# A fused attention and mixture-of-experts kernel: the identity in a tile of its own, other constants loaded later, and the first routing phase's PSUM and id tiles rearranged

## The chip, the core and the metric

One NeuronCore of a Trainium2 chip runs the program; the metric is the device time of one execution in microseconds (us). The engines are TensorE (PE in the profile, with its weight loads as PEld), VectorE (DVE), ScalarE (ACT), GpSimd (POOL) and SyncE (SP, which here issues most of the transfers).

## The reference

Three stages, in fp32:

```python
# 1. attention over a window of 64, B=4, H=8, S=576, D=64; x is (2304, 512)
scores = where(0 <= i - j < 64, q @ k.T / 8, -1e9)
x = softmax(scores) @ v
# 2. eight experts, each takes at most 288 tokens; all 2304*8 logits are
#    visited in falling order, a token goes to the first expert with room
logits = x @ w_gate
order = argsort(-logits.flatten())
out[mask_e] = relu(x[mask_e] @ w1[e]) @ w2[e]
# 3. a dense block with a leaky ReLU
h = out @ w_in
return maximum(0.01 * h, h) @ w_out
```

## The kernel before, in words

**Attention** (`attention`, lines 63 to 268) goes through 18 chunks of 128 tokens. One turn `i` of its main loop issues: `scores(i)` (mask products at line 121, then q times k at line 130, into the PSUM tile `as`), the row maxima on DVE (lines 137, 138), the gate products `stage_g` in every third turn (line 93, from the load `avt`), the exponentials on ACT (line 145), `values(i-2)` (line 165, into the PSUM tile `ao`; for the last two chunks into a tile of the tag `as`), `stage_gt` (transposes of the gate products against the identity, line 107; DVE copies them into the value tile `avo`, line 108, and POOL copies that into `ave`, lines 110 and 112), `sums(i-2)` (lines 170 to 176, then `done(c)`, then the normalisation at line 181), and `trans(i-1)` (transposes of the exponentials against the identity, line 150, copied out at line 152). For the last three chunks the normalisation runs on ACT, eight instructions for each chunk at line 185, as the last work of the stage.

The loads go out on SP in one written order. `early()` runs after the first two loads and `late()` after six. `early()` also starts the load of `cft`, all fp32 constants with the identity among them, on ACT's queue. `late()` issues two more constant loads (`cit`, and `cbt` beyond its first 128 columns) on SP, and calls `Router.start` (line 343). That puts seven small instructions into DVE's queue ahead of the first row maximum; three of them read constants: line 347 reads `cft`, line 349 reads `cft`, line 350 reads the late part of `cbt`. Every engine works through its own queue in order.

**Routing** (`Router`). The eight experts are filled in eight phases. Phase 0 finds its threshold digit by digit in six rounds. A round counts on PE how many logits lie above each candidate (19 small matmuls into a PSUM tile `rq`: one for what is left of the experts' room, 18 for the chunks, which multiply the comparison grid `r_G` by the one-hot choice `r_oh`), DVE clips the count (`r_sat`, a scan), PE sums it up (`rp`), and DVE builds the next comparisons (three instructions on `r_G`, then `r_E`). The first round's grid and one-hot are made ahead, chunk group by chunk group, in `ahead` (line 361; groups of 6, 6, 3 and 3 chunks), and so are the integer keys (`keys`, line 388; results `r_k`, `r_M`, `r_E`). `ahead` and `keys` are generators: two steps are taken per turn of the attention, the rest in one go at the end. After the six rounds phase 0 places the chosen tokens and turns slot numbers into row ids: two DVE products into `r_OB` (nine chunks each), after each of them nine matmuls into one PSUM tile, then `r_ip`, one matmul, and `r_ids`. Each matmul reads 128 columns of `r_OB` from its chunk's start on, that is beyond its own 18 columns.

The attention's PSUM pool has all eight banks: the tag `as` four, `apt` two and `ao` two. After it, `m_pa` (tag `acc`, four banks), `rps` (tag `rp`, one), `pm` (tag `xt`, one) and `m_ph` (two) take the banks over. Phase 0's counts are tiles of the tag `acc`.

**Experts and the dense block** (`Moe`). After phase 0's ids, three gathers fetch expert 0's rows (`xg`), PE runs warm-up products meanwhile (`warm`, `WARM`), transposes the rows (`xtp`) and starts expert 0. The later phases are interleaved with the matmuls by a planner in the program (`Clocks`, `RouteDriver`): it adds up modelled times for each engine, starting after the attention, and issues a routing or weight-conversion piece when the model says that its inputs are there. Whether expert 1's gather has been issued by step 6 (`self.soon`) decides if its rows are transposed beside expert 0's matmuls or only after a forced `R.finish(1)`.

Of the kernel before, what the change touches and what calls it, by code (L numbers as in the profile page):

```python
# [6 lines left out]
F32 = mybir.dt.float32  # L7
# [10 lines left out]
NT = 18  # L18
# [260 lines left out]
def consts_np():  # L279

    f, i, b = {}, {}, {}
    p = np.arange(128, dtype=np.float32)[:, None]
# [9 lines left out]
    f['tid'] = 128 * np.arange(18, dtype=np.float32) + p - IDC  # L292
    f['ident'] = np.eye(128, dtype=np.float32)
    j = np.arange(128)[:, None] % 18
# [18 lines left out]
class Router:  # L313
# [3 lines left out]
    def __init__(self, nc, pool, pp, L, cf, ci, cb, ones_b, pow2):  # L317
# [19 lines left out]
        self.G = [pool.tile([128, n * NT], BF, name=f"r_G{k}") for k, n in enumerate((128, 38))]  # L337
        self.OB = pool.tile([128, 18 * 17 + 128], F16, name="r_OB")
        for x in self.G + [self.OB]:
            nc.gpsimd.memset(x, 0.0)  # L340
        self.ip = pool.tile([128, 128], F16, name="r_ip")
    def start(self):
        v, cf = self.nc.vector, self.cf
        v.memset(self.base, 0.0)
        v.memset(self.sat, 0.0)
        v.memset(self.ip, 0.0)
        v.tensor_copy(self.uw, cf['ew'])
        v.memset(self.slotg, 0.0)
        v.tensor_scalar(out=self.nrem, in0=self.base[:, 0], scalar1=cf['na'], scalar2=cf['nb'], op0=ALU.mult, op1=ALU.add)
        v.tensor_copy(self.comb, self.combb)  # L350
    def ps(self, p, n, apart=False):

        self.nps += 1
        if apart:
            return self.p0.tile([128, 512], F32, tag="acc", name=f"rq{self.nps}", bufs=4)[:p, :n]
        return self.pp.tile([128, 128], F32, tag="rp", name=f"rp{self.nps}")[:p, :n]
# [3 lines left out]
    def ahead(self, a, b):  # L360

        v = self.nc.vector
        if a == 0:
            self.first = [self.t([128, NT], F32, "m", 0), self.t([128, NT, 8], BF, "oh", 0), self.t([128, NT], F32, "mxw", 0)]
            self.ge0, self.win0 = self.grid(0, 128)
            self.e0 = self.t([128, NT], F32, "E", 0)
            self.eqw0 = self.G[1].bitcast(F32)[:, :8 * NT].rearrange("p (c e) -> p c e", e=8)
        m, OH, mxw, eqw = self.first[0][:, a:b], self.first[1][:, a:b], self.first[2][:, a:b], self.eqw0[:, a:b]
        def b3(ap, last):
            return ap.unsqueeze(2).to_broadcast([128, b - a, last])  # L370
        def bm(ap, last):
            return ap.unsqueeze(1).to_broadcast([128, b - a, last])
        ks = self.keys(m, self.e0, a, b, True)
        v.tensor_reduce(out=m, in_=self.Lm[:, a:b], axis=AX.X, op=ALU.max)
        yield True
        v.tensor_tensor(out=eqw, in0=self.Lm[:, a:b], in1=b3(m, 8), op=ALU.is_equal)
        next(ks)
        yield True
        v.tensor_tensor(out=self.ge0[:, a:b, :127], in0=b3(m, 127), in1=bm(self.ci['t1'].bitcast(F32), 127), op=ALU.is_ge)
        next(ks)  # L380
        v.tensor_tensor(out=eqw, in0=eqw, in1=bm(self.cf['ew'], 8), op=ALU.mult)
        next(ks)
        yield True
        v.tensor_reduce(out=mxw, in_=eqw, axis=AX.X, op=ALU.max)
        next(ks)
        yield True
        v.tensor_tensor(out=OH, in0=eqw, in1=b3(mxw, 8), op=ALU.is_equal)
        next(ks)
    def keys(self, m, E, a, b, first):

# [14 lines left out]
        yield  # L405
        v.scalar_tensor_tensor(out=E[:, a:b], in0=M[:, 0], scalar=float(1 << 31), in1=M[:, 1], op0=ALU.add, op1=ALU.add)
        yield
    def grid(self, k, w):
# [3 lines left out]
    def phase(self, ph, out):  # L412
# [26 lines left out]
        if ph < 7:  # L439
            for r in range(6):  # L440
# [6 lines left out]
                for lo, hi in zip(cuts, cuts[1:]):  # L447
# [9 lines left out]
                    if hi == NT:  # L457
# [7 lines left out]
                        elif ph:  # L465
                            E = t([128, NT], F32, "E", f"{ph}_0")
                            for _ in self.keys(m, E, 0, NT, False):
                                pass
                        else:
                            E = self.e0  # L470
# [7 lines left out]
                yield 'v', 1  # L478
                v.tensor_tensor_scan(self.sat[rows], pc[rows], self.ones[rows, :8], 0.0, ALU.max, ALU.min)
                yield 'p', 0  # L480
                pa = self.ps(128, 8)
# [73 lines left out]
        yield 'd', 0  # L555
        OB = self.OB[:, :NT * NT].rearrange("p (c a) -> p c a", a=NT)
        HI = self.G[0].bitcast(F16)[:, :NT * NT].rearrange("p (c a) -> p c a", a=NT)
# [5 lines left out]
        pi = None  # L563
        for lo, hi in ((0, 9), (9, 18)) if ph == 0 else ((0, 18),):
            TT(out=OB[:, lo:hi], in0=HI[:, lo:hi], in1=b3(cf['tid'][:, lo:hi], hi - lo, NT), op=ALU.mult)
            yield 'p', 0
            pi = self.ps(128, 16) if pi is None else pi
            for c in range(lo, hi):
                nc.tensor.matmul(pi, self.OB[:, NT * c:NT * c + 128], LO[:, c], start=(c == 0), stop=(c == NT - 1))
        yield 'v', 1  # L570
# [775 lines left out]
def build(nc, tc, qT, kT, v, vT, wg, cfd, cid, cbd, w12, wio, out):  # L1346
    with ExitStack() as ctx:
        ctx.enter_context(tc.manual_schedule())
        c = ctx.enter_context(tc.tile_pool(name="c", bufs=1))
        dr = ctx.enter_context(tc.tile_pool(name="dr", bufs=1, space=bass.MemoryType.DRAM))  # L1350
        cft = c.tile([128, CFN], F32, name="cft")
        cit = c.tile([128, CIN], I32, name="cit")
        cbt = c.tile([128, CBN - MW], BF, name="cbt")
        cf = {k: cft[:, o:o + n] for k, (o, n) in CFO.items()}
        ci = {k: cit[:, o:o + n] for k, (o, n) in CIO.items()}
        cb = {k: cbt[:, o - MW:o - MW + n] for k, (o, n) in CBO.items()}
        ident = cf['ident']
        ones = c.tile([128, 128], BF, name="ones"); nc.vector.memset(ones, 1.0)

        nc.scalar.activation(cft[:, 0:1], ones[:, 0:1], AF.Exp)  # L1360
        L = c.tile([128, 160], F32, name="L")[:, :NT * 8].rearrange("p (c e) -> p c e", e=8)
# [26 lines left out]
        queue = []  # L1388
        def done(c):
            if c in ahead:  # L1390
                queue.append(rt.ahead(*ahead[c]))
            if c == NT - 1:
                drain()
# [3 lines left out]
        with tc.tile_pool(name="mk", bufs=1) as mk:  # L1397
# [4 lines left out]
            def early():  # L1402
                nc.scalar.dma_start(cft, cfd)
                nc.sync.dma_start(wg_sb, wg)
            def late():
                nc.sync.dma_start(cit, cid)
                nc.sync.dma_start(cbt[:, 128:], cbd[:, MW + 128:].bitcast(BF))
                rt.start()
            attention(nc, tc, ident, cb['ident'], qT, kT, v, vT, wg_sb, maskb, xd, L, filler, early, late, done)
        pa = ctx.enter_context(tc.tile_pool(name="m_pa", bufs=4, space=PSUM, reuse_waits="tile"))  # L1410
        rt.p0 = pa
        rt.pp = ctx.enter_context(tc.tile_pool(name="rps", bufs=1, space=PSUM, reuse_waits="tile"))
        pm = ctx.enter_context(tc.tile_pool(name="pm", bufs=1, space=PSUM, reuse_waits="tile"))
        ph = ctx.enter_context(tc.tile_pool(name="m_ph", bufs=2, space=PSUM, reuse_waits="tile"))
        nc = cv.nc = rt.nc = Clocks(nc)
# [33 lines left out]
```

## Time and profile before

| | us |
|---|---|
| runs of the kernel before | 780.02, 781.0, 3415.35 |
| their median | 781.0 |
| the profiled execution | 781.95 |
| its span, first to last instruction | 780.3 |
| outside the span (difference) | 1.65 |
| PE busy in the span | 735.5 (94%) |
| DVE busy | 438.3 (56%) |
| ACT busy | 334.8 (43%) |
| POOL busy | 173.2 (22%) |

In the rows further down the first number of a timeline or chain row is the start in us from the span's beginning, the second the duration in us (of a merged row: of all its instructions). In brackets stands how long the engine was idle before it, and what ended that. A name such as `as<-ak,aq` is output from inputs.

### The profile page before, as it was taken

Reading aid. Unit: us, or ns where it says so; the run is one execution under the profiler, and the core shown is the slowest. Engines: PE = TensorE matmul, PEld = TensorE weight load, DVE = VectorE, ACT = ScalarE, POOL = GpSimd, SP = SyncE. Lnnn points to the kernel's source line nnn. Section 1 sums busy time; section 2 is a strip of 40 time slices with the busy share of each in tenths; the row PEclk is TensorE's granted clock in tenths of the full one; section 3 lists DMA queues with packets and bytes.
Section 4 is the critical chain, followed back from the end, with each engine's and each line's share of the span. In section 5 each row is a group of like instructions: output and inputs, shape, how many; then the busy total and the mean of one; then the engine's idle time right before and its main releaser. Section 6 shows DMA issues by size and latency. Waiting matters only on the chain.

```text
span 780.3 us, 15243 instructions
## 1 busy us (share of the span) xinstructions
PE 735.5 (94%) x5906; PEld 624.5 (80%) x5906; DVE 438.3 (56%) x1113; ACT 334.8 (43%) x736; POOL 173.2 (22%) x262
## 2 busy tenths in 40 slices
PE   3999649999999999999999999999999999999996
PEld 2777526789777779997778899988889998888895
DVE  2689778989789979987752334222233222222332
ACT  2788824657775534432112445322134532222321
POOL 3434112402000004400000388300018850000201
PEclk9999959999999999999999999999999999999999
DMA  9997128643477556433224365623426452214742
GB/s 346 408 380 271 56 76 310 232 161 108 161 239 252 212 194 219 159 122 130 107 84 163 109 220 165 217 80 136 152 91 220 157 199 104 105 64 173 252 172 98
DMA packets 39943, 138.56 MB, mean 178 GB/s; under 512 B 4926, under 2 KB 5822, under 8 KB 39872
## 3 DMA queue, kind: packets, MB, share of 16 engines
q1 hardware_dynamic: 35136, 123.11, 44.1%
q0 software_dynamic: 4304, 14.16, 5.4%
q8 instruction: 46, 0.75, 0.4%
q10 hardware_dynamic: 432, 0.32, 0.1%
q14 instruction: 25, 0.20, 0.1%
HBM read 117.66 MB, written 19.92 MB: 176 GB/s over the span
## 4 chain that ended last, share of the span: by engine, by line
PE 74%; DVE 17%; DMA 4%; ACT 3%; issue 2%; POOLq 0%; SPq 0%; POOL 0%; DVEq 0%; ACTq 0%
PE h L1262 33%; PE oa L1262 21%; PE ya L1262 10%; DVE r_G L1262 3%; PE rp L1262 3%; DVE w L1262 2%; PE ao L165 2%; DMA cv_in<-in_wio_dram 2%; PE apt L150 1%; DVE cv_r L1262 1%; PE as L130 1%; DVE amx L137 1%; PE xtp L1262 1%; DMA cbt<-in_cb_dram 1%; DVE hh L1262 1%
## 5 line engine op out<-in xcount | busy, mean ns | idle before, releaser
L1262 PE MATMUL h<-Y,w 128*128 128x512 f32 (+1 forms) x600 | 135.2, 371 | 0.0
L1262 DVE SCALAR_TENSOR_TENSOR h<-h,tg 128x512 f32<-128x512 f32 (+1 forms) x80 | 51.6, 644 | 146.9 <-ACT tg L1262 146.7
L1262 PE MATMUL oa<-w,hh 128*128 128x512 f32 x540 | 132.9, 392 | 0.0
L1262 ACT COPY tg<-h 128x512 f32<-128x512 f32 (+1 forms) x80 | 43.5, 543 | 185.4 <-PE h L1262 172.9
L1262 PEld LDWEIGHTS h<-Y,w 128*128 128x128 f32 x600 | 104.3, 189 | 18.4
L1262 PEld LDWEIGHTS oa<-w,hh 128*128 128x128 f32 x540 | 99.7, 188 | 19.8 <-issue 0.2
L1262 POOL TENSOR_TENSOR w<-raw,w 128x512 fp32r<-128x512 f32 x53 | 66.7, 1290 | 206.6 <-DVE xT L1262 111.3
L1262 PE MATMUL ya<-hh,w 128*128 128x288 f32 x672 | 99.8, 296 | 0.6 <-DVE hh L1262 0.6
L1262 PE MATMUL h<-xT,w 128*128 128x288 f32 x672 | 100.0, 297 | 0.0
L1262 PEld LDWEIGHTS h<-xT,w 128*128 128x128 f32 x672 | 92.5, 188 | 0.6
L1262 PEld LDWEIGHTS ya<-hh,w 128*128 128x128 f32 x672 | 92.0, 188 | 0.8 <-DVE hh L1262 0.8
L1262 PE MATMUL h<-Y,res 128*128 128x512 f32 (+1 forms) x360 | 81.7, 371 | 0.0
L1262 PE MATMUL oa<-res,hh 128*128 128x512 f32 x324 | 80.6, 393 | 0.0
L1262 DVE TENSOR_TENSOR hh<-h,hh 128x512 fp32r<-128x512 f32 (+1 forms) x80 | 51.0, 637 | 38.5 <-ACT hh L1262 38.3
L1262 POOL DMA_INDIRECT out_dram<-ot,sidx x18 | 19.5, 1081 | 238.0 <-DVE ot L1262 134.9
L1262 PEld LDWEIGHTS h<-Y,res 128*128 128x128 f32 x360 | 62.5, 189 | 11.0
L1262 ACT CAST hh<-h 128x512 fp32r<-128x512 f32 (+1 forms) x80 | 43.5, 544 | 64.1 <-DVE h L1262 64.1
L1262 PEld LDWEIGHTS oa<-res,hh 128*128 128x128 f32 x324 | 59.5, 188 | 11.9 <-ACT hh L1262 0.4
L1262 ACT ACTIVATE hh<-h 128x288 fp32r<-128x288 f32 (+1 forms) x64 | 26.4, 412 | 91.7 <-PE h L1262 89.5
L1262 ACT CAST w<-raw 128x512 fp32r<-128x512 f32 x112 | 64.1, 620 | 0.0
L1262 DVE SCALAR_TENSOR_TENSOR hh<-h,hh 128x288 fp32r<-128x288 f32 x56 | 25.4, 454 | 63.4 <-ACT hh L1262 63.2
L145 ACT ACTIVATE ap<-as,anm 128x128 f32<-128x128 f32 x144 | 41.6, 396 | 24.3 <-DVE anm L138 16.8
(172 smaller groups left out, 941.5 us busy)
## 6 DMA issues: line engine op xcount, KB each, us to landing
w<-wsp SPq DMA_DIRECT2D x80, 512.0 KB, 3.4
raw<-in_w_dram SPq DMA_DIRECT2D x53, 512.0 KB, 3.9
cv_in<-in_wio_dram SPq DMA_DIRECT2D x32, 512.0 KB, 5.2
wsp<-w SPq DMA_DIRECT2D x20, 512.0 KB, 3.4
avo<-in_v_dram SPq DMA_DIRECT2D x6, 876.0 KB, 8.1
aq<-in_q_dram SPq DMA_DIRECT2D x12, 384.0 KB, 7.5
avt<-in_vt_dram SPq DMA_DIRECT2D x6, 768.0 KB, 8.0
xd<-ax SPq DMA_DIRECT2D x18, 256.0 KB, 7.2
```

The source lines that it names most:

```text
L130: nc.tensor.matmul(S[64 * t:64 * t + 64, a, u, :].rearrange("p (b c) -> p b c", b=2), q[h], k[h], start=False, stop=True, skip_group_check ...
L137: nc.vector.tensor_reduce(out=mx, in_=S[:, a:a + n], axis=AX.X, op=ALU.max)
L145: nc.scalar.activation(p[:, u, :], S[:, a, u, :], AF.Exp, bias=nm[a][:, u:u + 1], scale=0.125)
L150: nc.tensor.transpose(pt[:, u, :], p[:, u, :], ident)
L165: nc.tensor.matmul(o[64 * t:64 * t + 64, h // 4, h % 4, :], ptb[:, u, 64 * t:64 * t + 64], (ve, vo)[t][m][:, s, h, :], start=True, stop=Tr ...
L1262: return f(*a, **kw)
```

## The change

The identity becomes the first 128 columns of the fp32 constants and gets a tile `ident`, which `early()` loads; the other 183 columns stay in `cft` and are loaded in `late()` on SP, between `cit` and `cbt`. `start` keeps only memsets; the three instructions that read constants move to `start2`, called in `sums(4)` by `done(4)`, after chunk 4's logits. In `ahead` the steps of `keys` come later (two of them after `r_oh`), and the last one, which made `r_E` by chunk groups, becomes `rest`: one instruction over all 18 chunks, issued in phase 0's first round behind the scan. Phase 0's counts use the tag `xt` of the pool `pm`. `r_OB` becomes two tiles, and phase 0 puts its first nine chunks into the one and the other nine into the other.

```diff
-    f, i, b = {}, {}, {}
+    f, i, b = {'ident': np.eye(128, dtype=np.float32)}, {}, {}
...
-        self.OB = pool.tile([128, 18 * 17 + 128], F16, name="r_OB")
-        for x in self.G + [self.OB]:
+        self.OB = [pool.tile([128, 18 * (n - 1) + 128], F16, name=f"r_OB{n}") for n in (9, 18)]
+        for x in self.G + self.OB:
             nc.gpsimd.memset(x, 0.0)
...
         v.memset(self.ip, 0.0)
+        v.memset(self.slotg, 0.0)
+    def start2(self):
+        v, cf = self.nc.vector, self.cf
         v.tensor_copy(self.uw, cf['ew'])
-        v.memset(self.slotg, 0.0)
         v.tensor_scalar(out=self.nrem, ...
         v.tensor_copy(self.comb, self.combb)
...
-            return self.p0.tile([128, 512], F32, tag="acc", name=f"rq{self.nps}", bufs=4)[:p, :n]
+            return self.p0.tile([128, 4, 96], F32, tag="xt", name=f"rq{self.nps}", bufs=1).rearrange("p a b -> p (a b)")[:p, :n]
...
         v.tensor_tensor(out=eqw, in0=self.Lm[:, a:b], in1=b3(m, 8), op=ALU.is_equal)
-        next(ks)
         yield True
         v.tensor_tensor(out=self.ge0[:, a:b, :127], ...
-        next(ks)
+        yield True
...
         v.tensor_tensor(out=OH, in0=eqw, in1=b3(mxw, 8), op=ALU.is_equal)
+        yield True
         next(ks)
+        next(ks)
...
-        v.scalar_tensor_tensor(out=E[:, a:b], in0=M[:, 0], scalar=float(1 << 31), in1=M[:, 1], op0=ALU.add, op1=ALU.add)
-        yield
+    def rest(self, E):
+        self.nc.vector.scalar_tensor_tensor(out=E, in0=self.M[:, 0], scalar=float(1 << 31), in1=self.M[:, 1], op0=ALU.add, op1=ALU.add)
...
                 v.tensor_tensor_scan(self.sat[rows], ...
+                if ph + r == 0:
+                    self.rest(E)
...
-        for lo, hi in ((0, 9), (9, 18)) if ph == 0 else ((0, 18),):
-            TT(out=OB[:, lo:hi], in0=HI[:, lo:hi], ...
+        for k, (lo, hi) in enumerate(((0, 9), (9, 18)) if ph == 0 else ((0, 18),)):
+            ob = self.OB[(k + (ph > 0)) % 2]
+            TT(out=ob[:, :NT * (hi - lo)].rearrange("p (c a) -> p c a", a=NT), in0=HI[:, lo:hi], ...
...
-                nc.tensor.matmul(pi, self.OB[:, NT * c:NT * c + 128], LO[:, c], ...
+                nc.tensor.matmul(pi, ob[:, NT * (c - lo):NT * (c - lo) + 128], LO[:, c], ...
...
+            if c == 4:
+                rt.start2()
...
-                nc.scalar.dma_start(cft, cfd)
+                nc.scalar.dma_start(ident, cfd[:, :128])
                 nc.sync.dma_start(wg_sb, wg)
             def late():
                 nc.sync.dma_start(cit, cid)
+                nc.sync.dma_start(cft, cfd[:, 128:])
                 nc.sync.dma_start(cbt[:, 128:], cbd[:, MW + 128:].bitcast(BF))
...
-        rt.p0 = pa
...
+        rt.p0 = pm
```

## Rows read from the trace of the kernel before

**Rows 1.** Windows: us, then busy us of each engine, clock, DMA share, GB/s.
```profile
10.71:16.15 5.44, 0.85 (x8) 0.16 (x9) 1.99 (x4) 0.42 (x2) 0.00 (x0) 1.00 1.02 410
16.15:22.98 6.83, 5.91 (x64) 4.41 (x66) 1.48 (x4) 5.26 (x18) 3.08 (x5) 0.50 1.01 410
...
95.80:115.00 19.20, 6.92 (x142) 5.61 (x142) 14.36 (x57) 6.36 (x14) 1.40 (x2) 0.50 0.15 54
...
123.50:780.30 656.80, 645.05 (x4228) 555.56 (x4227) 351.24 (x845) 258.75 (x508) 130.44 (x185) 1.00 0.47 162
```

**Rows 2.** Timeline of DVE at the start of the attention.
```profile
14.13 0.17 DVE L350 CAST r_comb<-cbt 128x3 f16<-128x3 bf16 x1 [4.91 <-DMA cbt<-in_cb_dram]
14.21 1.22 DVE L137 TENSOR_REDUCE amx<-as 128x8 f32<-128x1024 f32 x1
```

**Rows 3.** Tile `as`, PE, 6 to 8.4 us: ns min/median/max, first and last start.
```profile
L130 PE MATMUL as<-ak,aq x32: 417/417/418, 6.7 to 8.2; 64*64 64x128 f32 x32
```

**Rows 4.** The chain that ended last, 0 to 150 us: start, us, what.
```profile
18.32 0.91 PE agt L107 x12
...
22.55 1.39 PE ao L165 x32
...
24.97 0.34 PE as L121 x4
25.31 0.87 PE as L130 x32
...
26.97 1.17 PE ao L165 x32
...
31.55 0.35 PE agt L107 x12
...
37.80 0.85 PE ag L93 x8
...
56.88 0.59 PE apt L150 x4
```

**Rows 5.** Timeline of POOL at the start of the attention.
```profile
19.70 0.66 POOL L110 COPY ave<-avo 64x584 f32<-64x584 f32 x1 [10.51 <-DVE avo L108]
```

**Rows 6.** Timeline of SP: the third load of `avt`.
```profile
17.70 0.33 SPq L86 DMA_DIRECT2D avt<-in_vt_dram  x1
```

**Rows 7.** Tile `avt` in the window of that one issue.
```profile
DMA to landing us min/median/max: 12.5/12.5/12.5
```

**Rows 8.** Timelines of ACT, DVE and PE, end of attention and phase 0.
```profile
92.40 4.96 ACT L185 ACTIVATE ax<-ao,ari 128x64 f32<-128x64 f32 x24
...
93.33 0.18 DVE L387 TENSOR_TENSOR r_oh<-r_G,r_mxw 128x24 bf16<-128x24 f32 x1
...
95.77 0.17 PE L1262 MATMUL rq<-r_nrem,r_sel 128*128 128x8 bf16 x1 [4.83 <-ACT ax L185]
...
96.46 0.17 DVE L1262 TENSOR_TENSOR_SCAN r_sat<-rq,ones 127x8 bf16<-127x8 f32 x1 [2.86 <-PE rq L1262]
96.89 1.07 DVE L1262 SCALAR_TENSOR_TENSOR r_G<-r_E,rp,cft 128x279 bf16<-128x279 f32 x3 [0.26 <-PE rp L1262]
...
98.31 0.18 DVE L1262 TENSOR_TENSOR_SCAN r_sat<-rq,ones 31x8 bf16<-31x8 f32 x1 [0.19 <-PE rq L1262]
```

**Rows 9.** Timeline of DVE at the end of phase 0.
```profile
112.95 0.33 DVE L1262 TENSOR_TENSOR r_OB<-r_G,cft 128x162 f16<-128x162 f16 x1
113.79 0.33 DVE L1262 TENSOR_TENSOR r_OB<-r_G,cft 128x162 f16<-128x162 f16 x1 [0.51 <-PE rp L1262]
```

**Rows 10.** Timelines of PE and DVE: expert 0's start, and phase 1.
```profile
114.97 4.29 PE L1262 MATMUL warm<-cbt 128*128 128x512 bf16 x11
...
120.36 0.55 PE L1262 MATMUL xtp<-cft,xg 96*128 96x96 f32 x4 [1.10 <-DMA xg<-xd,r_ids]
...
143.85 0.16 DVE L1262 TENSOR_SCALAR r_ids<-rp 96x3 int32<-96x3 f32 x1 [0.38 <-PE rp L1262]
...
159.05 0.83 PE L1262 MATMUL xtp<-cft,xg 96*128 96x96 f32 x8
```

More of the change, by code (lines that the diff above doesn't have):

```diff
@@ L292, in consts_np @@
     f['tid'] = 128 * np.arange(18, dtype=np.float32) + p - IDC
-    f['ident'] = np.eye(128, dtype=np.float32)
     j = np.arange(128)[:, None] % 18
@@ L372, in bm @@
             return ap.unsqueeze(1).to_broadcast([128, b - a, last])
-        ks = self.keys(m, self.e0, a, b, True)
+        ks = self.keys(m, a, b, True)
         v.tensor_reduce(out=m, in_=self.Lm[:, a:b], axis=AX.X, op=ALU.max)
@@ L387, in ahead, with keys @@
         v.tensor_tensor(out=OH, in0=eqw, in1=b3(mxw, 8), op=ALU.is_equal)
+        yield True
         next(ks)
-    def keys(self, m, E, a, b, first):
+        next(ks)
+    def keys(self, m, a, b, first):
         v, w = self.nc.vector, b - a
@@ L466, in phase @@
                             E = t([128, NT], F32, "E", f"{ph}_0")
-                            for _ in self.keys(m, E, 0, NT, False):
+                            for _ in self.keys(m, 0, NT, False):
                                 pass
+                            self.rest(E)
                         else:
@@ L479, in phase @@
                 v.tensor_tensor_scan(self.sat[rows], pc[rows], self.ones[rows, :8], 0.0, ALU.max, ALU.min)
+                if ph + r == 0:
+                    self.rest(E)
                 yield 'p', 0
@@ L555, in phase @@
         yield 'd', 0
-        OB = self.OB[:, :NT * NT].rearrange("p (c a) -> p c a", a=NT)
         HI = self.G[0].bitcast(F16)[:, :NT * NT].rearrange("p (c a) -> p c a", a=NT)
@@ L563, in phase @@
         pi = None
-        for lo, hi in ((0, 9), (9, 18)) if ph == 0 else ((0, 18),):
-            TT(out=OB[:, lo:hi], in0=HI[:, lo:hi], in1=b3(cf['tid'][:, lo:hi], hi - lo, NT), op=ALU.mult)
+        for k, (lo, hi) in enumerate(((0, 9), (9, 18)) if ph == 0 else ((0, 18),)):
+            ob = self.OB[(k + (ph > 0)) % 2]
+            TT(out=ob[:, :NT * (hi - lo)].rearrange("p (c a) -> p c a", a=NT), in0=HI[:, lo:hi], in1=b3(cf['tid'][:, lo:hi], hi - lo, NT), op=ALU.mult)
             yield 'p', 0
@@ L568, in phase @@
             for c in range(lo, hi):
-                nc.tensor.matmul(pi, self.OB[:, NT * c:NT * c + 128], LO[:, c], start=(c == 0), stop=(c == NT - 1))
+                nc.tensor.matmul(pi, ob[:, NT * (c - lo):NT * (c - lo) + 128], LO[:, c], start=(c == 0), stop=(c == NT - 1))
         yield 'v', 1
@@ L1350, in build @@
         dr = ctx.enter_context(tc.tile_pool(name="dr", bufs=1, space=bass.MemoryType.DRAM))
-        cft = c.tile([128, CFN], F32, name="cft")
+        ident = c.tile([128, 128], F32, name="ident")
+        cft = c.tile([128, CFN - 128], F32, name="cft")
         cit = c.tile([128, CIN], I32, name="cit")
         cbt = c.tile([128, CBN - MW], BF, name="cbt")
-        cf = {k: cft[:, o:o + n] for k, (o, n) in CFO.items()}
+        cf = {k: cft[:, o - 128:o - 128 + n] for k, (o, n) in CFO.items()}
         ci = {k: cit[:, o:o + n] for k, (o, n) in CIO.items()}
         cb = {k: cbt[:, o - MW:o - MW + n] for k, (o, n) in CBO.items()}
-        ident = cf['ident']
         ones = c.tile([128, 128], BF, name="ones"); nc.vector.memset(ones, 1.0)
-        nc.scalar.activation(cft[:, 0:1], ones[:, 0:1], AF.Exp)
+        nc.scalar.activation(ident[:, 0:1], ones[:, 0:1], AF.Exp)
         L = c.tile([128, 160], F32, name="L")[:, :NT * 8].rearrange("p (c e) -> p c e", e=8)
```

## The prediction

> **What bounds the kernel now.** I read the windows by stage first. From 123.5 us to the end PE is busy 645.05 of 656.80 us at the full clock (2.4 GHz) [rows 1]; nothing of the change touches that work, and what can be won there is small. The stretch before it is different: PE is busy 0.85 of the 5.44 us from 10.71 on, 5.91 of the next 6.83 but at a granted clock of 0.50 (1.2 GHz), and 6.92 of the 19.20 us of phase 0 [rows 1]. So I went to DVE's timeline for the first hole, to the chain that ended last for what followed it, and to the timelines of ACT, DVE and PE for the last one.
>
> The first hole: chunk 0's scores end at 8.2 + 0.42 = 8.62 us [rows 3], but the first row maximum starts at 14.21, behind the copy at line 350, which sat 4.91 us until the late constants had landed [rows 2]. All of the attention hangs on that maximum: exponentials, transposes, next scores. The last hole: phase 0's first count could start once `r_oh` is there (93.33 + 0.18 = 93.51 us), but waited until 95.77 for ACT, which was normalising the last chunks [rows 8]; its PSUM bank held their outputs. From there to the gathers everything is one chain of small instructions.
>
> **The change part by part.** The sum is made on the profiled execution (span 780.3 us, 781.95 with what lies around it).
>
> *Constants off DVE's queue.* Without the three constant readers the first maximum can follow the scores after the lag of any DVE instruction behind PE; I allow 0.1 us, so 8.7 instead of 14.21: 5.5 us earlier. Then the chain repeats itself: exponentials, the gate copy, the `agt` products at 18.32 [rows 4], now at 12.8. Of what must happen before that, the gate products (0.85 us, all the work of the first hole [rows 1]) and the first transposes (0.59 [rows 4]) need 1.44 of the 2.1 us between 10.71 and 12.8. POOL's extra memset of the small `r_OB` tile lies in 10.51 us of idle time [rows 5], which shrinks by 5.5. The three moved instructions come in chunk 6's turn, where PE carries the chain; I cost them at nothing, and at most at 0.5 us if DVE were late there. SP's queue gets one more issue, before the loads of chunk 3 and later; the DMA share is already 1.02 [rows 1], so bytes, not issues, set when these land.
>
> *The clock.* PE ran at half clock from 16.15 to 22.98, after the stretch with 0.85 busy of 5.44 [rows 1]. The chain's PE pieces from 18.32 to the end of `ao` at 22.55 + 1.39 = 23.94 took 5.62 us. The same pieces later, at the full clock, take 0.35 (`agt`) + 0.59 (`apt`) + 0.34 and 0.87 (`as`) + 1.17 (`ao`) = 3.32 [rows 4]. With the hole closed PE has work from 10.7 on nearly without a break, so I expect the clock to stay up: another 2.3 us. The Trainium skill says the same of such holes (TensorE: Matmul & The Clock Gate, "HAM oscillation — how this bites in real kernels"): idle gaps between bursts send the engine back to half rate, and each burst then starts slow. By that rule the 2.3 us are won, by its opposite they are not; the trace agrees with it here [rows 1].
>
> *What is late next.* 5.5 + 2.3 = 7.8 us earlier, chunk 6's gate products would start at 37.80 - 7.8 = 30.0 [rows 4]. Their load lands at 17.70 + 12.5 = 30.2 [rows 6, 7], and with the DMA engines full [rows 1] it can't land earlier: moving 91.5 KB of constants (183 columns of 4 bytes on 128 partitions) from ahead of these loads to between them changes nothing in the total. So the front gains 0.2 to 0.3 less: 7.5 us. This is the bound from above; from below it is 5.5 less the 0.5 us for the moved instructions, 5.0, if the clock falls all the same.
>
> *`ahead` and `rest`.* Three instructions fewer on DVE in sum, two of them moved behind the last `r_oh`; `rest` runs behind the first scan, in the gap of 0.26 us in which DVE waits for PE [rows 8]. `r_oh` comes about 0.2 us sooner (two places of some 0.1 us, the pitch of its neighbours); the rest I set to nothing (bounds -0.3 to +0.3).
>
> *Counts in another bank.* `pm` is opened after `m_pa` (four banks, as many as the tag `as`) and `rps`, so I take its bank to be one of `apt`, last read by a copy before the last values. Then the first count waits for `r_oh` alone, and 15 of its 18 chunk products can run before. In later rounds the scan starts 98.31 - 97.96 = 0.35 us after the last comparison (96.89 + 1.07 = 97.96) [rows 8]. So the scan comes at 93.51 - 0.2 + 0.35 = 93.66 instead of 96.46 [rows 8]: 2.8 us. If all 19 products run after `r_oh`, the lag is 96.46 - 95.77 = 0.69 and the gain 2.46. If the bank is that of `ao`, the first eight of the 24 normalisations hold it, until 92.40 + 4.96 / 3 = 94.05; then the scan comes at 94.05 + 0.69 = 94.74, a gain of 1.7. Nothing new is queued behind: one buffer is enough, since a round needs the last one's digit.
>
> *Ids in two tiles.* The second product on `r_OB` waited 0.51 us for the first nine matmuls [rows 9]. In a tile of its own it runs beside them; the second nine then follow the first nine at once, and the idle time less a lag of 0.1 goes: 0.4 us (bounds 0 and 0.5).
>
> Sum: 7.5 + 2.8 + 0.4 = 10.7 us, 781.95 - 10.7 = 771.25 for an execution like the profiled one. The two runs near it, 780.02 and the median 781.0, lie 0.95 to 1.93 below 781.95, so I forecast 770.5. That is 1.3% below 781.0, and about 2% is what a measurement of this kernel can tell from no change.
>
> **The rivals.**
>
> *The clock falls anyway.* The gain at the front is 5.5 instead of 7.5 and the time 772.5. For it: PE has short breaks between 10.7 and 12.8. Against: it went low only after a stretch with 5.44 - 0.85 = 4.6 us of idle time [rows 1].
>
> *The loads become the bound.* The DMA share is 1.01 to 1.02 in the windows where the work moves forward [rows 1]; a load that lands after its new need takes the wait's place. For it: the margin at the third `avt` load is gone. Against: it is one load; of the others I show no rows, and take them to land in time. If chunk 6's turn and those behind it wait up to 4 us more, the sum is 6.7 and the time 774.5. The skill (DMA: Bandwidth & Descriptors, "Issuing engines are not separate DMA queues") says that transfers of all queues run on the same 16 engines and interleave, so no reordering of constants makes room. By that rule an early landing is not to be had and a late one is possible; no row here contradicts it.
>
> *The count's wait stays*, by the bank of `ao` or by a wait that I don't see. Gain 0 to 1.7 in place of 2.8, time 771.6 to 773.3.
>
> *The clock returns late for expert 0.* It was low through phase 0, 95.80 to 115.00 [rows 1]; `warm` brings it back, and the transposes follow 120.36 - 114.97 = 5.4 us after it began [rows 10]. The page on the clock gate (Part 1) says that the monitor runs free of the program, so a shifted program can meet it at another place. If half clock lasts into transposes and first products, it costs about as much as the front's low stretch, 2.3 us: 772.8.
>
> *Slower: expert 1's rows come too late for the short way.* The planner starts from other modelled times after phase 0. If it has not issued expert 1's gather by step 6, the kernel takes the branch with `R.finish(1)`, and PE stands through the rest of that routing and the way from ids to first product, 123.5 - 114.97 = 8.5 us as in phase 0 [rows 1, 10]. It is slower than before from 10.7 - 8.5 = 2.2 us of routing left; with 4 us left, 781.95 - 10.7 + 12.5 = 783.8. Against it: `r_ids` of phase 1 is there at 143.85, and the transposes of step 6 run at 159.05 [rows 10], a margin of 15 us against a change in modelled times of a few tenths.
>
> **How the numbers follow.** Forecast 0.56; clock falls 0.13; loads bind 0.12; count's wait stays 0.09; late clock 0.06; slower branch 0.02; the other 0.02 for a larger gain. Predicted is the forecast's 770.5. The range takes the four milder rivals and, below, 3 us for waits that I overlooked: 767.5 to 776.0. Over 2% faster means under 765.4, which no case reaches: 0.02. Over 2% slower means above 796.6: 0.01. Within 2%: 0.97.
>
> **What would show it.** Right: the first maximum near 8.7 us with no DMA wait before it; clock 1.00 without a fall until the end of the attention; chunk 3's mask products near 17.5 instead of 24.97; the first scan of phase 0 about 2.8 us earlier against `r_oh` less 0.2, and no `rq` wait on ACT; the two `r_OB` products back to back; the windows of the experts as long as before (656.8 us to the end). Wrong: new PE or DVE waits on `avt`, `aq` or `ak` before 40 us; a half clock after 16 us; `rq` still released by ACT; or a tail that is longer than 656.8 by more than 2 us.

## The result and the profile after

The changed kernel took 773.16 us (median of four runs, 772.07 to 773.66) against 780.86 us for the kernel before on the same chip (median of four, 780.02 to 781.0 and one disturbed run of 3415.35): a ratio of 0.9903 without the disturbed run, interval 0.9884 to 0.9923. That is 1% less, inside the range of the prediction and 2.7 us above its point. In the profiled pair the span went from 780.3 to 770.4 us, 9.9 us less, and the execution from 781.95 to 772.07; the first of these lies above the other undisturbed runs of the kernel before and the second is the fastest of the changed one, so between the medians the gain is less, 7.7 us.

The first view is the windows of the kernel after: the two stretches of the first hole, phase 0 (the window of [rows 1] moved 9.6 us earlier), and everything from expert 0's first product on. The columns are those of [rows 1].

```profile
10.71:16.15 5.44, 4.89 (x97) 3.24 (x92) 2.37 (x4) 4.54 (x16) 1.85 (x3) 1.00 1.03 404
16.15:22.98 6.83, 6.50 (x136) 5.02 (x135) 5.01 (x14) 6.51 (x22) 2.16 (x4) 1.00 1.02 411
86.20:105.40 19.20, 6.95 (x127) 5.36 (x128) 15.39 (x66) 8.90 (x27) 1.44 (x3) 0.57 0.21 74
112.34:770.40 658.06, 647.84 (x4228) 555.26 (x4227) 351.18 (x845) 259.00 (x508) 129.91 (x185) 1.00 0.48 162
```

Against [rows 1], PE's busy time in the first stretch is 4.89 us instead of 0.85, and the granted clock, which was 0.50 in the second, is 1.00 in both. The last row is the surprise: with the same 4228 matmuls, PE is busy 2.8 us longer than before, 647.84 against 645.02 to 645.05, and the stretch is 1.3 us longer (658.06 against 656.77).

The timelines of DVE and PE of the kernel after show the milestones in order: the first row maximum, chunk 2's gate transposes, chunk 3's mask products and gate products, and the last value sum (`asm`).

```profile
8.61 1.23 DVE L137 TENSOR_REDUCE amx<-as 128x8 f32<-128x1024 f32 x1 [7.31 <-PE as L130]
...
12.92 0.57 PE L107 MATMUL agt<-ident,agb 128*64 128x64 f32 x12
...
17.57 0.41 PE L121 MATMUL as<-maskb,cbt 64*64 64x512 bf16 x4
...
19.19 0.85 PE L93 MATMUL ag<-avt,wg_sb 128*32 128x384 f32 x8 [0.33 <-DMA avt<-in_vt_dram]
...
83.92 0.17 DVE L170 TENSOR_SCALAR asm<-ao 128x8 f32<-128x8 f32 x1 [0.27 <-PE ao L165]
```

The rows of the kernel before that the last sum and the ids further down are compared with:

```profile
90.99 0.17 DVE L170 TENSOR_SCALAR asm<-ao 128x8 f32<-128x8 f32 x1 [0.48 <-PE ao L165]
...
115.15 0.16 DVE L1262 TENSOR_SCALAR r_ids<-rp 96x3 int32<-96x3 f32 x1 [0.28 <-PE rp L1262]
```

The first maximum comes at 8.61 instead of 14.21 [rows 2], 5.60 us earlier. The gate transposes at 12.92 were at 18.32, a gain of 5.40; at chunk 3's mask products, 17.57 instead of 24.97 [rows 4] and past the stretch that ran at half clock before, it is 7.40, and at the last `asm`, which stood at 90.99 before, it is 7.07. A load that nobody waited for at this place before has become visible: chunk 3's gate products wait 0.33 us for `avt`. The load was issued at 9.57 us and landed 9.5 us later; before the change it was issued at 8.76 and landed 8.9 us later, well ahead of its products at 26.12. Two more waits on loads are new before that: 0.32 us of PE on `ak` at 9.69 and 1.27 us of DVE on `avo` at 13.77.

Now phase 0, the same view of the kernel after: the first count's products, `r_oh`, the first scan, and the end with the two `r_OB` products and the ids.

```profile
83.84 0.52 PE L1267 MATMUL rq<-r_oh,r_G 128*128 128x8 bf16 x15
86.12 0.18 DVE L387 TENSOR_TENSOR r_oh<-r_G,r_mxw 128x24 bf16<-128x24 f32 x1
86.35 0.22 PE L1267 MATMUL rq<-r_oh,r_G 128*128 128x8 bf16 x3 [1.99 <-DVE r_oh L387]
86.61 0.17 DVE L1267 TENSOR_TENSOR_SCAN r_sat<-rq,ones 127x8 bf16<-127x8 f32 x1
86.70 0.16 DVE L1267 SCALAR_TENSOR_TENSOR r_E<-r_M 128x18 f32<-128x18 int32 x1
87.04 1.07 DVE L1267 SCALAR_TENSOR_TENSOR r_G<-r_E,rp,cft 128x279 bf16<-128x279 f32 x3 [0.18 <-PE rp L1267]
...
103.07 0.56 DVE L1267 TENSOR_TENSOR r_OB<-r_G,cft 128x162 f16<-128x162 f16 x2
104.66 0.16 DVE L1267 TENSOR_SCALAR r_ids<-rp 96x3 int32<-96x3 f32 x1 [0.28 <-PE rp L1267]
```

In [rows 8] the count waited for ACT until 95.77; here 15 of the 18 chunk products are done before `r_oh`, the last three follow `r_oh` alone, and the scan starts 2.69 us behind the last `asm`, where it took 96.46 - 90.99 = 5.47: 2.78 us gained. `rest` (the `r_E` row) sits in the gap behind the scan. The two `r_OB` products of [rows 9] are now one merged row of 0.56 us, and the ids follow 104.66 - 103.07 = 1.59 us after their start instead of 2.20 (they came at 115.15): 0.61 us gained.

So the ids come 115.15 - 104.66 = 10.49 us earlier (7.07 + 2.78 + 0.61, and 0.03 on the way); from ids to expert 0's first product it takes 7.68 us instead of 8.38, and the rest is 1.29 us longer: 10.49 + 0.70 - 1.29 = 9.9 us.

**Where the rest got longer.** The groups of instructions on the page of the kernel after, those of the dense block by the tile that holds the weights:

```profile
L1267 PE MATMUL h<-Y,w 128*128 128x512 f32 (+1 forms) x600 | 135.3, 371 | 0.0
L1267 PE MATMUL oa<-w,hh 128*128 128x512 f32 x540 | 133.0, 392 | 0.0
...
L1267 PE MATMUL h<-Y,res 128*128 128x512 f32 (+1 forms) x360 | 82.8, 374 | 0.0
L1267 PE MATMUL oa<-res,hh 128*128 128x512 f32 x324 | 82.2, 398 | 0.0
```

The same groups of the page before:

```profile
L1262 PE MATMUL h<-Y,w 128*128 128x512 f32 (+1 forms) x600 | 135.2, 371 | 0.0
L1262 PE MATMUL oa<-w,hh 128*128 128x512 f32 x540 | 132.9, 392 | 0.0
...
L1262 PE MATMUL h<-Y,res 128*128 128x512 f32 (+1 forms) x360 | 81.7, 371 | 0.0
L1262 PE MATMUL oa<-res,hh 128*128 128x512 f32 x324 | 80.6, 393 | 0.0
```

The dense block's weights come in two kinds of SBUF tiles: `w`, filled again and again, and `res`, which are written once and stay. In the `h` products they are the stationary operand against `Y`, in the `oa` products the moving one against `hh`. Only the products that read `res` changed: 81.7 + 80.6 = 162.3 us became 82.8 + 82.2 = 165.0, 2.7 us for 684 products. The chain that ended last shows it per group of twelve; first a stretch of the dense block after:

```profile
494.61 2.83 PE oa L1267 x12
497.44 2.80 PE h L1267 x12
500.24 2.72 PE oa L1267 x12
502.96 2.72 PE h L1267 x12
505.68 2.80 PE oa L1267 x12
```

The same view of the kernel before, from the same place of the block on:

```profile
506.12 2.79 PE oa L1262 x12
508.92 2.72 PE h L1262 x12
511.64 2.72 PE oa L1262 x12
514.36 2.72 PE h L1262 x12
517.08 2.72 PE oa L1262 x12
```

Group by group, 2.79, 2.72, 2.72, 2.72 and 2.72 us have become 2.83, 2.80, 2.72, 2.72 and 2.80. The clock is 1.00 in both, the order of the matmuls is the same, and PE waits for nobody here. What the change did to these tiles is to move some of them: the new small tile `r_OB9` has 18 * 8 + 128 = 272 values of 2 bytes, 544 bytes on each partition, and it is allocated behind `res` and ahead of `Y`, `hh` and `w`. So the two operands of a product with `res` stand further apart, while those of a product with `w` have moved together. The first theory that I tested is that this distance decides the pace. Its rival is that the longer time is a matter of the execution or of the changed timing before it, not of addresses.

### The profile page after: what moved, and what is told of

Read it like the earlier page. It is cut to its first block, busy times and chain, and to the rows that moved or that the text cites. A ratio compares the mean times of both kernels' runs of the same rounds, so it can differ in the third digit from the quotient of the medians.

```text
span 770.4 us, 15241 instructions
## 1 busy us (share of the span) xinstructions
PE 735.4 (95%) x5905; PEld 622.3 (81%) x5906; DVE 437.9 (57%) x1110; ACT 335.5 (44%) x736; POOL 172.9 (22%) x263
## 4 chain that ended last, share of the span: by engine, by line
PE 78%; DVE 14%; DMA 4%; issue 2%; ACT 1%; SPq 0%; POOLq 0%; POOL 0%; DVEq 0%; ACTq 0%
PE h L1267 35%; PE oa L1267 24%; PE ya L1267 10%; DVE r_G L1267 3%; PE rp L1267 3%; PE ao L165 2%; DVE w L1267 2%; DMA cv_in<-in_wio_dram 1%; DMA avt<-in_vt_dram 1%; PE apt L150 1%; DVE amx L137 1%; PE xtp L1267 1%; DMA ak<-in_k_dram 1%; PE as L130 1%; PE warm L1267 1%
## 5 line engine op out<-in xcount | busy, mean ns | idle before, releaser
L1267 PE MATMUL h<-Y,w 128*128 128x512 f32 (+1 forms) x600 | 135.3, 371 | 0.0
L1267 PE MATMUL h<-Y,res 128*128 128x512 f32 (+1 forms) x360 | 82.8, 374 | 0.0
L1267 PE MATMUL oa<-res,hh 128*128 128x512 f32 x324 | 82.2, 398 | 0.0
```

What stands on the lines that cost most here:

```text
L1267: return f(*a, **kw)
```

## The experiments

Where nothing else is said the ratio is against the kernel before on the same chip; three chips were used, on which the kernel before takes 781, 785 and 786 us, so ratios and stages are compared, not microseconds across chips. A "shift" is how many bytes on each partition the tiles behind `res` stand further from it than in the kernel before.

**The distance: four kernels.** In the changed kernel, 32 bytes more (shift 576):

```diff
-        self.OB = [pool.tile([128, 18 * (n - 1) + 128], F16, name=f"r_OB{n}") for n in (9, 18)]
+        self.OB = [pool.tile([128, 18 * (n - 1) + 128 + 16 * (n == 9)], F16, name=f"r_OB{n}") for n in (9, 18)]
```

> The changed kernel with its small id tile 32 bytes larger, so that every tile behind it (Y, hh, the streamed weights) again stands to the resident weights res as it did before the change. Placement theory: the twelve products of a step with weights from res come back from 2.80 to 2.72 us, PE busy in the two res groups falls from 82.8 + 82.2 to about 81.7 + 80.6 us, and the time falls by 2 to 3 us against the changed kernel (near 771 us). Rival, that PE was only running differently in that execution: the groups stay near 165 us and the time near 773 us.

Measured: 777.62 against 785.93 us, 0.9911 (0.9880 to 0.9942). The `res` groups stayed at 82.7 + 82.2 us. The recovery didn't come. But the expectation has its premise wrong: with 32 bytes more the tiles stand 576 bytes further from `res` than before the change, not as before it. So this run speaks neither for nor against the distance.

In the kernel before, 32 bytes more in `r_OB` (shift 32):

```diff
-        self.OB = pool.tile([128, 18 * 17 + 128], F16, name="r_OB")
+        self.OB = pool.tile([128, 18 * 17 + 128 + 16], F16, name="r_OB")
```

> The kernel before with 32 bytes added to its id tile and nothing else. Placement theory: the res groups rise from 162.3 to about 165 us of PE busy, 2.80 us for twelve, and the time rises by 2 to 3 us over before (783 us). Rival: nothing changes, 781 us.

Measured: 788.32 against 785.93, 1.0032 (1.0008 to 1.0055), slower by padding alone. The page's groups of this kernel:

```profile
L1262 PE MATMUL h<-Y,res 128*128 128x512 f32 (+1 forms) x360 | 82.9, 374 | 0.0
```

With the `oa` group at 82.1 that is the 165.0 us of the changed kernel, although not one instruction of the work differs. The rival falls.

In the kernel before, the same 32 bytes ahead of `res`, so that `res` and all behind it move together (shift 0):

```diff
-        L = c.tile([128, 160], F32, name="L")[:, :NT * 8].rearrange("p (c e) -> p c e", e=8)
+        L = c.tile([128, 168], F32, name="L")[:, :NT * 8].rearrange("p (c e) -> p c e", e=8)
```

> The kernel before with 32 bytes added ahead of res, so that res and everything behind it move together. If the distance of weights and moving data to each other decides (placement theory), the res groups stay at 162.3 us and the time at 781 us. If the place of the moving data alone decides, res products take 2.80 us for twelve as in the changed kernel and the time rises by 2 to 3 us.

Measured: 785.87 against 785.93, 1.0002 (0.9987 to 1.0017), the groups at 81.7 + 80.6 as before. So what counts is how far the tiles behind `res` stand from it, and not their place alone. All of them moved together in these runs, so they do not separate the distance of a product's own two operands from that of `res` to another tile in use. For the operands speaks that the products with `w`, whose operands moved together, took 135.1 to 135.3 and 132.9 to 133.4 us in all the kernels.

In the kernel before, 128 bytes more (`+ 64` values; shift 128):

> The kernel before with 128 bytes added to its id tile. If the distance between weights and moving data has to be a multiple of 128 bytes, the res groups stay at 162.3 us and the time is that of before. If of 256 bytes, they rise to about 165 us and the time by 2 to 3 us.

Measured: 787.69 against 785.12, 1.0030 (1.0015 to 1.0045), groups at 82.9 + 82.0. A multiple of 128 isn't enough.

**The change with a distance of 768 bytes.** The small tile padded from 544 to 768 bytes (three times 256), run twice:

```diff
-        self.OB = [pool.tile([128, 18 * (n - 1) + 128], F16, name=f"r_OB{n}") for n in (9, 18)]
+        self.OB = [pool.tile([128, 18 * (n - 1) + 128 + 112 * (n == 9)], F16, name=f"r_OB{n}") for n in (9, 18)]
```

> The changed kernel with its small id tile 224 bytes larger, so that everything behind it stands 768 bytes further than before the change instead of 544 (576 in the first try). Placement theory with a unit of 128 or 256 bytes: the two res groups fall from 165 to about 162.3 us of PE busy, 2.72 us for twelve, and the time falls by 2 to 3 us against the changed kernel, to a ratio to before of about 0.987. Rival, any shift behind res costs it: 165 us, ratio 0.990.

Measured: 775.40 against 785.12, 0.9868 (0.9840 to 0.9897). The page's groups of this kernel:

```profile
L1267 PE MATMUL h<-Y,res 128*128 128x512 f32 (+1 forms) x360 | 81.7, 371 | 0.0
L1267 PE MATMUL oa<-res,hh 128*128 128x512 f32 x324 | 80.6, 393 | 0.0
```

> The same kernel as after_768, for the three that stand beside it here: the changed kernel with everything behind res 768 bytes further than before the change. Ratio to before near 0.987, last asm near 84 to 85 us, first scan 2.7 us behind it.

Measured: 771.28 against 781.02, 0.9882 (0.9864 to 0.9899), the groups at 81.7 + 80.5. From the first `h<-Y` to the end it takes 585.50 us; the kernel before needed 585.92 and the changed one 587.58. On the other two chips this stretch is longer, 587.6 to 589.8 us in the kernels at the short pace of the groups and 590.1 to 591.8 in those at the long one (one execution of each). The last `asm` came at 84.12; in the profiled execution of the first set, on another chip, it came at 85.06, so one kernel can differ by 0.9 us there.

In sum, shifts of 0 and 768 bytes run at the short pace (162.2 to 162.3 us for the 684 products) and 32, 128, 544 and 576 at the long one (164.9 to 165.0). All fit a multiple of 256; a shift of just 256 wasn't run, and why the distance matters to PE isn't shown.

**The front alone.** The kernel before with `ident` in its own tile, the late constants and `start2`, and nothing else:

```diff
+        ident = c.tile([128, 128], F32, name="ident")
+        cft = c.tile([128, CFN - 128], F32, name="cft")
...
+            if c == 4:
+                rt.start2()
...
-                nc.scalar.dma_start(cft, cfd)
+                nc.scalar.dma_start(ident, cfd[:, :128])
...
+                nc.sync.dma_start(cft, cfd[:, 128:])
```

> The kernel before with the start of the change alone: identity in its own tile, other constants later, the three readers behind chunk 4. Theory: the first maximum at 8.6 us, no half clock until the end of the attention, the last sums (last asm on DVE, 90.99 before) 7.0 us earlier, the rest as before, so 774 us. Rival, the front's gain needs the other parts or is given back in the DVE-bound half of the attention: under 5 us, 776 us or more.

Measured: 777.23 against 785.93, 0.9905 (0.9878 to 0.9932). The first maximum comes at 8.55, the windows of the first hole have PE busy and the clock full:

```profile
10.71:16.15 5.44, 5.32 (x104) 3.66 (x98) 2.53 (x4) 4.61 (x16) 2.00 (x4) 1.00 1.03 408
16.15:22.98 6.83, 6.69 (x138) 5.08 (x134) 4.84 (x14) 6.64 (x23) 2.01 (x3) 1.00 1.04 416
```

The last `asm` is at 83.44, 7.55 us earlier than before. The count still waits as in [rows 8], as PE's timeline of this kernel shows:

```profile
88.24 0.17 PE L1263 MATMUL rq<-r_nrem,r_sel 128*128 128x8 bf16 x1 [4.85 <-ACT ax L185]
```

The ratio of the front alone is that of the whole change, 0.9905 against 0.9903. So in the time of the whole change one sees nothing of what the count's bank and the ids bring; that fits what the second tile costs.

**The clock alone.** The kernel before, its hole left as it is, but filled with 16 products that nobody reads:

```diff
+            if i == 1:
+                dm = pp.tile([128, 2, 512], F32, tag="ao", name="hole", bufs=1)
+                for _ in range(16):
+                    nc.tensor.matmul(dm[:, 0], identb, maskb, start=True, stop=True)
```

> The kernel before with 16 added products of 128x512 on PE (their result is not used) in the hole between the first gate products and the first transposes, the wait on the constants left as it is. Clock theory: PE keeps the full clock after 16.15 us, the last asm comes about 2.3 us earlier (88.7 instead of 90.99) and the time falls by as much. Rival, the half clock there lies beside waits that rule anyway: under 1 us earlier.

Measured: 784.48 against 785.12, 0.9996 (0.9977 to 1.0014). The windows of the same stretches:

```profile
10.71:16.15 5.44, 4.55 (x28) 1.64 (x24) 1.91 (x4) 0.34 (x2) 0.00 (x0) 1.00 1.03 409
16.15:22.98 6.83, 5.68 (x100) 4.39 (x104) 3.12 (x9) 5.88 (x22) 3.33 (x5) 1.00 1.03 412
```

The clock doesn't fall, and chunk 2's `asm` comes at 30.25 instead of 32.22, 1.97 us earlier, against the 2.3 reckoned. But the gain doesn't reach the end: the last `asm` is at 91.72. On the way the chain that ended last shows stretches in which PE waits for nothing that the profile knows:

```profile
35.72 0.94 issue
...
42.69 0.30 issue
...
63.32 1.29 issue
```

Together they are 2.5 us; in the other kernels' chains between 25 and 85 us single ones of at most 0.57 us occur. What makes them is open. So the clock's term is shown at its place, not at the end: by its time this run fits its rival, under 1 us. That the gain reaches the end is read from the front alone, where the maximum comes 14.21 - 8.55 = 5.66 us earlier and the last `asm` 7.55.

**The count's bank alone.** The kernel before, with the counts in the tag `xt` of `pm`:

```diff
-            return self.p0.tile([128, 512], F32, tag="acc", name=f"rq{self.nps}", bufs=4)[:p, :n]
+            return self.p0.tile([128, 4, 96], F32, tag="xt", name=f"rq{self.nps}", bufs=1).rearrange("p a b -> p (a b)")[:p, :n]
...
-        rt.p0 = pa
...
+        rt.p0 = pm
```

> The kernel before with phase 0's counts in the tag xt of pm, and nothing else. Theory: the first scan of phase 0 comes about 2.9 us after the last asm instead of 5.47 (the last r_oh is still behind its key steps), a gain of 2.5 us in all, 778.4 us on a chip where before takes 780.9, and no rq wait on ACT. Rival, the wait only moves (another reader of the bank, or the next round's wait on ACT): under 1 us.

Measured: 782.38 against 785.12, 0.9967 (0.9950 to 0.9984), 2.7 us less. DVE's timeline of this kernel at the first count:

```profile
93.31 0.18 DVE L387 TENSOR_TENSOR r_oh<-r_G,r_mxw 128x24 bf16<-128x24 f32 x1
...
93.80 0.17 DVE L1262 TENSOR_TENSOR_SCAN r_sat<-rq,ones 127x8 bf16<-127x8 f32 x1 [0.21 <-PE rq L1262]
```

The last `asm` is at 90.96, so the scan stands 2.84 us behind it instead of 5.47. In this execution a later round's scan (at 102.02) waits 1.01 us for its count where the others wait 0.19, so that the ids come at 113.31, only 1.84 us earlier; what made that one late is open, and the time of the ten runs shows the whole gain.

**Without the reordering.** The changed kernel with 768 bytes, but `ahead` and `keys` as in the kernel before and no `rest`:

```diff
-        ks = self.keys(m, a, b, True)
+        ks = self.keys(m, self.e0, a, b, True)
...
-                if ph + r == 0:
-                    self.rest(E)
```

> As after_768, but with ahead, keys and the last key step in the order of the kernel before (no rest). Theory, that the longer list of steps in the DVE-bound half of the attention costs what it saves later: the last asm comes 0.4 to 0.6 us earlier than in after_768, the first scan 2.9 instead of 2.7 us behind it, in sum 0.2 to 0.4 us faster. Rival, the order of those steps is worth what it was made for: the last asm as in after_768 and the time 0.2 us longer.

Measured: 772.37 against 781.02, 0.9896 (0.9877 to 0.9915), with after_768_again at 0.9882 beside it: no difference that can be told. In the timeline `r_oh` follows the last `asm` (83.94) by 2.34 us, and the scan by 2.83; with the reordering (after_768_again) by 2.21 and 2.70. The reordering brings 0.13 us. The earlier last `asm` of the theory came to 0.18 us, less than one kernel differs by itself. The ids came 10.92 us before the first product, 2.63 us more than in after_768_again. Of these, 1.45 lie ahead of the transposes: the first gather of expert 0's rows took 5.9 us from issue to landing instead of 4.4. The other 1.18 follow behind them, with the granted clock at 0.60, 0.50, 0.50 and 0.69 in the four microseconds from 112 on. The same is shown with its rows under the last version below.

**The late constants on ACT's queue.** The changed kernel with 768 bytes and

```diff
-                nc.sync.dma_start(cft, cfd[:, 128:])
+                nc.scalar.dma_start(cft, cfd[:, 128:])
```

The theory was that the one issue more on SP delays the load for which chunk 3's gate products wait.

> As after_768, but the rest of the constants is loaded on ACT's queue instead of SP's. Theory, that the one issue more on SP holds back every load behind it: the second avt load is issued near 8.8 us as before the change instead of 9.6, lands a good 1 us earlier, chunk 1's sums come 0.3 us or more earlier, and the time falls by 0.3 to 0.5 us. Rival, only bytes count: the landing and the time stay.

Measured: 772.93 against 781.02, 0.9901 (0.9886 to 0.9916). The `avt` load was issued at 9.53 us instead of 9.57 (9.17 in after_768_again), the one before it at 6.06 instead of 4.65, and the last `asm` came at 84.95. Nothing is won. But the edit also moves the load: on ACT's queue it goes out at 2.78 us instead of 6.84, so its bytes now go ahead of the first `avt`. The run therefore doesn't test the issue by itself; it gives the theory no support, and it doesn't refute it. The traces agree with what the Trainium skill says of loads issued on several engines (DMA: Bandwidth & Descriptors, "Issuing engines are not separate DMA queues"): they share the same DMA engines, and a second issuer saves the issuing time alone. With a DMA share of 1.02 to 1.04 in all these windows, it is more likely the bytes ahead of them than the issuing that the loads wait for.

**Both together**, as the attempt at a best version: no reordering, constants on ACT's queue, 768 bytes.

> noreorder_768 with the rest of the constants on ACT's queue, that is both of the edits above. By the two theories 0.5 to 0.9 us faster than after_768, ratio to before near 0.986; by the two rivals the time of after_768 or 0.2 us more.

Measured: 772.41 against 781.02, 0.9886 (0.9870 to 0.9902); not to be told from after_768_again. Its profiled execution (774.57) shows another thing. The last `asm` is early, at 83.67, and the ids come at 104.60, but the first product only at 116.74, 12.1 us later. PE's timeline of this kernel:

```profile
105.23 2.90 PE L1263 MATMUL warm<-cbt 128*128 128x512 bf16 x9 [0.22 <-issue]
111.19 0.88 PE L1263 MATMUL xtp<-ident,xg 96*128 96x96 f32 x4 [3.07 <-issue]
...
116.74 0.57 PE L1263 MATMUL h<-xT,w_raw 128*128 128x288 f32 x1
```

and the windows around it, where PE stands idle after `warm` and the clock is low when the transposes begin:

```profile
108.00:110.00 2.00, 0.12 (x1) 0.00 (x0) 2.00 (x3) 0.00 (x0) 2.00 (x4) 1.00 1.00 268
110.00:112.00 2.00, 0.81 (x5) 0.83 (x6) 1.29 (x5) 0.00 (x0) 1.72 (x4) 0.56 0.93 246
112.00:114.00 2.00, 2.00 (x8) 0.98 (x7) 0.00 (x0) 0.48 (x1) 0.00 (x0) 0.50 1.02 391
114.00:116.00 2.00, 2.00 (x29) 1.71 (x28) 0.46 (x2) 0.80 (x2) 0.00 (x0) 0.50 1.01 408
```

The transposes read the gathered rows (tile `xg`). From issue to landing its three gathers take in this kernel, and below that in after_768_again:

```profile
DMA to landing us min/median/max: 5.4/5.7/6.1
...
DMA to landing us min/median/max: 4.0/4.2/4.4
```

The first gather is the slowest of the three in both. Here it goes out at 105.04 and lands at 105.04 + 6.1 = 111.14 us, and the transposes start at 111.19; in after_768_again it is 105.34 + 4.4 = 109.74 and 109.86, in the kernel before 115.59 + 4.7 = 120.29 and 120.36 [rows 10]. So the 3.07 us that the row puts down to "issue" end with the gather, as the 1.10 us before the change do. Against after_768_again the way from ids to first product is 3.85 us longer: 1.63 until the transposes begin, and 2.22 behind them, where the clock, fallen while PE stood idle, is at half. Why the gathers take longer here isn't shown.

**The version with the lowest time.** The changed kernel with the small tile padded to 768 bytes has the lowest time: 771.28 us at 781.02 before, against 773.16 at 780.86 for the change as it stands. Its ratios, 0.9868 and 0.9882, lie below the change's 0.9903, but the intervals overlap, so the times by themselves don't settle it; what speaks for it is that the pad takes the `res` groups back by 2.7 us, and that 32 or 128 bytes cost the kernel before 0.3% in runs whose intervals exclude no change.

## Why the prediction was right, and which step failed

- *Constants off DVE's queue*, 5.5 us: measured 5.60 (8.61, forecast 8.7).
- *The clock*, 2.3 us: it doesn't fall, in any kernel that closes the hole, nor in the one that fills it; the rival "the clock falls anyway" is out. At its place the change gave 7.40 - 5.40 = 2.00 and the fill 1.97, so the term was 0.3 too large. The trace agrees here with the section of the Trainium skill that the prediction named (TensorE: Matmul & The Clock Gate, "HAM oscillation — how this bites in real kernels"), that idle gaps bring the clock down: behind the gap with PE busy 0.85 of 5.44 us the clock was 0.50, and with the gap closed (4.89) or filled (4.55) it was 1.00.
- *The front in all*, 7.5 by the bound of a load: 7.55 in the front alone, 7.07 in the whole change. The load that became visible was one `avt` load sooner than I said, that of chunk 3's gate products: it lands at 19.05, 1.4 us later than before the change, and costs 0.33 us at 19.19. Chunk 6's gate products, at 30.85 where I had 30.2, follow `aptb` of ACT. With that and the wait on `ak` a sign that the prediction had set for being wrong, new waits on `avt` or `ak` before 40 us, did come, in a size that cost tenths. Two executions of after_768 differ by 0.9 us here, so 0.4 more or less is not put down to an edit. As a cause of 4 us more, "the loads become the bound" is out.
- *`ahead` and `rest`*, nothing in sum: `r_oh` 0.13 us sooner (forecast 0.2), `rest` free, in the gap behind the scan; no difference in time.
- *Counts in another bank*, 2.8: measured 2.78 in the whole change, 2.63 (5.47 to 2.84) alone; the difference of 0.15 belongs to the reordering (0.13 in the run without it), which I had put into the same sum. 15 of 18 products ran early, as said. "The count's wait stays" is out.
- *Ids in two tiles*, 0.4 with bounds 0 and 0.5: measured 0.61, 0.1 over the upper bound; the two products together are also 0.1 us shorter (0.56 against twice 0.33). This is read from the whole change only: no run has the change without the second tile.
- *The slower rival*, expert 1's rows too late: the order of PE's matmuls is that of before, and no branch with `R.finish(1)` ran.

Up to the ids that is 10.49 where the sum said 10.7. The step that failed is the other side of the ids edit. I priced the second `r_OB` tile as a memset of POOL in idle time, and wrote of the experts that "nothing of the change touches that work"; the mark for being right, windows "as long as before (656.8 us to the end)", was missed by 1.3 us. Nobody reads that tile there, but it moves the others: 544 bytes aren't a multiple of 256, and 684 products pay 2.7 us of PE time, of which 1.3 to 1.7 us reached the profiled span and 2.4 to 2.6 us the medians (0.3% in the two padded kernels before). That is about the 2.7 us by which the point was low; with the pad the whole change brings 781.02 - 771.28 = 9.7 us. The remaining microsecond to 10.7 is of the size of the next point. The 0.70 us between ids and first product were in no term of the sum; that they came out in its favour was luck. The point itself had a slip, too: it took 0.75 off 771.25, although the two runs that it went by lie 0.95 to 1.93 lower, which would have given 769.3 to 770.3, further from the result.

*The clock returns late for expert 0* didn't occur in the change, but in two other kernels. From ids to the first product the profiled executions took 8.38 us (before) and 7.68 (after); in twelve of the fourteen traces it is 7.59 to 8.58, and in noreorder_768 and best 10.92 and 12.14. What the rival lacked is the first half of that delay: a late gather, behind which the clock is low. Both are kernels without the reordering, but so are all those built on the kernel before, with 7.59 to 8.58; and the profiled execution of best is the slowest of its four (774.57, the fastest 771.44). So it looks like a matter of single executions more than of the edit; with one trace for each kernel that isn't settled. It may be behind spreads such as 770.67 to 773.82, which wasn't shown either.

## What to carry to other kernels

Read the first and the last idle stretch of the bounding engine, and ask of each instruction at the head of a queue whether its input could be a smaller and earlier load; here three small constant readers and one PSUM tag cost some 10 us of 781. Where a change adds or resizes an SBUF tile, look at which tiles move, and compare the busy time of product groups that the change doesn't touch: 2.7 us were hidden there under a gain of 10. A size that brings the old pace back, here 768 bytes more instead of 544, is the version to try beside it. And where an engine's idle time is put down to "issue", compare its end with the landing of the load or gather that the next instruction reads.

## What the runs showed of the hardware that I had not expected

The pace of these matmuls (fp32r operands, 128 x 512) depends on how far their resident operand `res` stands in SBUF from the tiles behind it, the other operand among them: twelve take 2.72 us at a shift of 0 or 768 bytes and up to 2.80 in part of the groups at 32, 128, 544 and 576; moving all of them by 32 changes nothing. And PE can stand for 0.30 to 1.29 us in the middle of a group of products (before_warm), with no releaser that the profile shows; what it waits for is open.
